# Bias rows on another DMA queue, and eight PSUM banks for the first 1024 tokens of a gated SSM + MLP kernel

## The chip, the cores and the metric

The kernel runs on one core of a Trainium2 chip. The metric is device time in microseconds (us). Every execution whose state the record gives is fast; one of 578.97 us, the first of the kernel before, is in no ratio.

In the views of the profile, PE is TensorE at its matmuls, PEld TensorE loading weights, DVE is VectorE, ACT ScalarE, POOL GpSimd and SP SyncE; a `q` behind a name is that engine's sequencer, here issuing loads. `L632` is line 632 of that run's kernel.py, and `x14` a count of instructions. A load (DMA) is issued by one of the engines and lands when its data has arrived. TensorE writes its tiles into PSUM, which the kernel uses as eight banks; to evict a tile is to copy it out of its bank, which is then free again.

## The reference

For `x` of 2048 tokens by 640 channels the kernel computes `g * a + (1 - g) * b`:

```
g = sigmoid((x * gate_w).sum(-1))
a: state space model; Lam_bar = exp(exp(log_dt) * Lam), complex, 640 states
   Bu = x @ B_bar.T ;  h_t = Lam_bar * h_{t-1} + Bu_t ;  a = 2 * Re(h @ C.T) + x * Dskip
b: MLP; gelu(x @ w1 + b1) @ w2 + b2        with w1 640 x 1728, w2 1728 x 640
```

The inputs and the output are bf16.

## The kernel before

A small list scheduler orders the instructions of each engine when the kernel is built; each operation names what it reads and writes, and waits are emitted from that. It works on 512 tokens at a time (`q` = 0 to 3). TensorE does the first layer (`m1`, lines L632 for the first seven tiles, L654 and L658 for the others), the projections to the states (`bproj`, L687), the second layer (`m2`, L762) and the output projection (`cproj`, L786). ScalarE evicts the tiles from PSUM (`ge`, L640 and L667, and `u`, L696). VectorE does the scan. The part that the change touches, with cuts marked:

```python
BK_IN = [0, 1, 2, 3]      # banks of the tiles of m1 and bproj
BK_M2 = [4, 5]
BK_C = [6, 7]
# ... cut ...
op("b1z", "pool", 0.2, (), ["b1a", ("b1b", 0), ("b1b", 1)], f_b1z, prio=-50)   # zeroes b1rows
# lre, lim, ldt (rows of the SSM's parameters) are loaded on "act"
load("b1a", "pool", "l_b1a", b1rows[0:NF - 1, :], B_b1[0:nmain]..., ["b1a"], prio=-49, dur=0.8, lat=4.0)
for h in range(2):
    load(f"b1b{h}", "pool", f"l_b1b{h}", b1rows[NF - 1:NF, ...], B_b1[nmain:F]..., [("b1b", h)], prio=-48, dur=0.8, lat=4.0)
# ... cut ...
def f_colb():             # bias rows -> columns, by a transpose on TensorE in bank 7
    return inc("pe", nc.tensor.transpose(psD[:, 0:NF], b1rows[:, :], ident[0:NF, 0:NF]))
op("colb", "pe", 0.1, ["b1a", ("b1b", 0), ("b1b", 1), "ident"], [("bank", 7)], f_colb, prio=14.5)
# ... cut: m1_first does 7 tiles of q = 0 in banks 0 to 6, 5 matmuls of 512 columns each ...
def m1(q, j0=0):
    for jf in range(j0, NF):
        bank = BK_IN[ctr["in"] % 4]
        ctr["in"] += 1
        # ... 5 matmuls into PS[bank]; then ScalarE: GELU with bias b1col -> Gl ...
def bproj(q):
    for k in range(KP):
        for ci in range(2):
            bank = BK_IN[ctr["in"] % 4]
            ctr["in"] += 1
            # ... 5 matmuls with BT into PS[bank]; then ScalarE: copy -> U ...
# ... cut ...
m1_first(); m1(0, NW); bproj(0); ssm(0); gates(0); m1(1); ssm(1); bproj(1); ...; outs(0)
```

SyncE's queue carries, in this order, two loads of `x`, five of `W1sb` (one per 128 rows, the first seven tiles' columns), ten transposing loads of `BT` (the real and the imaginary half of each of five blocks of 128 rows), then `xT`, `W2sb` and `CT`.

## Time and profile before

| | before |
|---|---|
| median of the first three runs | 218.63 us (217.95 to 578.97) |
| span of the profile | 216.5 us |
| TensorE busy, granted clock | 98%, 1.00 |
| first-layer matmuls start | 6.64 us |
| last TensorE work ends | 213.9 us |

The page of the kernel before: engines' busy time in us, then the busy share of TensorE and its granted clock in 40 slices (9 is 90% or more), then the chain that ended last, by engine.

```profile
PE 211.3 (98%) x1288; PEld 124.0 (57%) x1299; DVE 191.2 (88%) x268; ACT 100.2 (46%) x173; POOL 6.3 (3%) x17
...
PE   7899999999999999999999999999999999999995
...
PEclk9999999999999999999999999999999999999999
...
PE 95%; DMA 2%; SPq 0%; issue 0%; ACT 0%; DVE 0%
```

TensorE works without a break once it has started; only the first slice and the last are below 80%. The granted clock reads 9 in every slice and 1.00 as a mean. PE shows 1288 instructions and PEld 1299: eleven matmul records are missing from this trace.

The head of that chain, in order of time (start us, us, what):

```profile
1.77 4.74 DMA W1sb<-in_B_w_dram
...
6.64 3.18 PE ps L632 x14
```

So the first load of `W1sb`, issued at 1.77 us and landing at 6.51, releases the first layer.

The timeline of TensorE (start us, us, engine, line, operation, count, and in brackets the idle time before and what ended it):

```profile
6.64 3.18 PE L632 MATMUL ps<-xT,W1sb 128*128 128x512 bf16 x14 [0.64 <-DMA W1sb<-in_B_w_dram]
9.76 0.18 PE L450 MATMUL ps<-ident,b1rows 14*128 14x14 bf16 x1
...
14.41 6.64 PE L654 MATMUL ps<-xT,W1sb 128*128 128x512 bf16 x30
20.98 0.74 PE L658 MATMUL ps<-xT,W1sb 128*64 128x256 bf16 x10
21.88 10.74 PE L687 MATMUL ps<-xT,BT 128*128 128x512 bf16 x49 [0.16 <-ACT Gl L667]
...
58.05 2.21 PE L762 MATMUL ps<-W2sb,Gl 128*128 128x320 bf16 x15
```

The bias transpose (L450) stands at a fixed place, after 14 matmuls. The groups follow each other at the pace of their matmuls: thirty of 512 columns take 6.57 us from start to start, 219 ns each with the change to the next form. The only wait for ScalarE in this listing is the 0.16 us before the projections.

The waits (who waits for whom: us in total, times, longest):

```profile
ACT U L696 <- PE ps L687: 18.6, 40, 0.6
...
ACT Gl L667 <- PE ps L654: 16.1, 41, 0.5
...
PE ps L687 <- ACT Gl L667: 0.2, 1, 0.2
```

ScalarE waits for TensorE's tiles 81 times on the two eviction lines; TensorE waits for an eviction once.

ScalarE's timeline around its first activation and the first GELU:

```profile
2.01 1.28 ACT L460 ACT_TABLE_LOAD   x1 [2.01 <-issue]
5.37 0.21 ACT L460 ACTIVATE dtb<-lcol 128x5 bf16<-128x5 f32 x1 [2.08 <-DVE lcol L444]
...
10.23 1.28 ACT L640 ACT_TABLE_LOAD   x1 [0.76 <-DVE b1col L455]
13.32 1.27 ACT L640 ACTIVATE Gl<-ps,b1col 128x512 bf16<-128x512 f32 x2 [1.81 <-PE ps L632]
```

The GELU table is ready at 11.5 us and the first GELU waits 1.8 us more for TensorE.

### The profile page before, as it was taken

What the parts mean: (1) busy time and instruction counts of PE and PEld (TensorE: products, weight loads), DVE (VectorE), ACT (ScalarE), POOL (GpSimd) and SP (SyncE); (2) the same over time, 40 slices, a digit from 0 to 9 for tenths busy, and PEclk for the clock granted to TensorE, in tenths of its full rate; (3) what the DMA queues carried; (4) which work ended last, traced back from release to release, by engine and by line L of the source; (5) the groups of instructions that cost most, each with busy time, mean ns of one, the idle gap of its engine ahead of it and who ended that gap; (6) DMA issues with size and microseconds to landing.
All of it is one profiled execution on the core that took longest, in us unless ns stands there. A gap on an engine that the chain in (4) does not pass through costs nothing.

```text
span 216.5 us, 3305 instructions
## 1 busy us (share of the span) xinstructions
PE 211.3 (98%) x1288; PEld 124.0 (57%) x1299; DVE 191.2 (88%) x268; ACT 100.2 (46%) x173; POOL 6.3 (3%) x17
## 2 busy tenths in 40 slices
PE   7899999999999999999999999999999999999995
PEld 4344444444577776444467777444457777777773
DVE  3799999999999999999997999799999989996312
ACT  2568656675533324556643233556673233232220
POOL 4000030000000100000000010000000000000000
PEclk9999999999999999999999999999999999999999
DMA  6997599996300040000000013000000000000000
GB/s 192 275 283 125 85 304 301 178 154 131 71 3 30 30 154 0 30 0 0 3 0 11 22 46 137 30 3 0 0 3 0 30 33 0 30 30 33 30 30 30
DMA packets 28923, 15.44 MB, mean 71 GB/s; under 512 B 22126, under 2 KB 28462, under 8 KB 28910
## 3 DMA queue, kind: packets, MB, share of 16 engines
q1 hardware_dynamic: 26912, 11.88, 23.7%
q0 software_dynamic: 656, 2.30, 3.5%
q10 hardware_dynamic: 1342, 1.07, 1.7%
q8 instruction: 10, 0.16, 0.3%
q14 instruction: 3, 0.02, 0.0%
HBM read 7.38 MB, written 2.62 MB: 46 GB/s over the span
## 4 chain that ended last, share of the span: by engine, by line
PE 95%; DMA 2%; SPq 0%; issue 0%; ACT 0%; DVE 0%
PE ps L762 28%; PE ps L654 22%; PE ps L786 20%; PE ps L687 20%; PE ps L632 4%; DMA W1sb<-in_B_w_dram 2%; PE ps L658 1%; SPq L328 0%; ACT Gl L667 0%; DVE osb L819 0%; PE ps L450 0%
## 5 line engine op out<-in xcount | busy, mean ns | idle before, releaser
L762 PE MATMUL ps<-W2sb,Gl 128*128 128x320 bf16 x448 | 63.6, 299 | 0.0
L762 PEld LDWEIGHTS ps<-W2sb,Gl 128*128 128x128 bf16 x448 | 43.6, 98 | 17.5 <-issue 0.4
L654 PE MATMUL ps<-xT,W1sb 128*128 128x512 bf16 x219 | 48.4, 379 | 0.3
L786 PE MATMUL ps<-CT,H 128*128 128x320 bf16 x320 | 46.1, 299 | 0.0
L727 DVE TENSOR_TENSOR_SCAN W<-atab,V 128x1280 bf16<-128x1280 f32 x16 | 44.3, 2811 | 0.3
L687 PE MATMUL ps<-xT,BT 128*128 128x512 bf16 x196 | 43.1, 379 | 0.3 <-ACT Gl L667 0.2
L786 PEld LDWEIGHTS ps<-CT,H 128*128 128x128 bf16 x320 | 31.2, 98 | 12.3
L667 ACT ACTIVATE Gl<-ps,b1col 128x512 bf16<-128x512 f32 x45 | 30.6, 692 | 16.1 <-PE ps L654 16.1
L654 PEld LDWEIGHTS ps<-xT,W1sb 128*128 128x128 bf16 x225 | 22.0, 98 | 26.5
L687 PEld LDWEIGHTS ps<-xT,BT 128*128 128x128 bf16 x200 | 19.4, 98 | 23.2 <-issue 0.4
L696 ACT ACTIVATE U<-ps 128x512 bf16<-128x512 f32 x40 | 23.9, 597 | 18.6 <-PE ps L687 18.6
L805 DVE SCALAR_TENSOR_TENSOR xg<-xn,gcol,dsk 128x640 bf16<-128x640 bf16 x16 | 13.9, 883 | 0.4
L770 ACT ACTIVATE E_0<-ps,g1col 128x320 bf16<-128x320 f32 x12 | 6.3, 527 | 16.5 <-PE ps L762 16.5
L611 DVE SCALAR_TENSOR_TENSOR scr<-xn,gwb 128x640 bf16<-128x640 bf16 x16 | 13.2, 823 | 0.4
L506 DVE TENSOR_TENSOR H<-H,V 128x1280 bf16<-128x1280 bf16 x16 | 12.5, 821 | 0.3
L506 DVE TENSOR_TENSOR V<-V,W 128x1280 bf16<-128x1280 bf16 x16 | 12.5, 821 | 0.3
L506 DVE TENSOR_TENSOR V<-mr,U 128x2560 bf16<-128x2560 bf16 x8 | 11.9, 1489 | 0.5 <-DVE s L506 0.3
L506 DVE TENSOR_TENSOR H<-c,W 128x2560 bf16<-128x2560 bf16 x8 | 11.9, 1488 | 0.1
L506 DVE TENSOR_TENSOR V<-s,W 128x2560 bf16<-128x2560 bf16 x8 | 11.9, 1484 | 0.0
L506 DVE TENSOR_TENSOR W<-mi,U 128x2560 bf16<-128x2560 bf16 x8 | 11.9, 1484 | 0.0
L770 ACT ACTIVATE E_2<-ps,g1col 128x320 bf16<-128x320 f32 x10 | 5.3, 527 | 13.4 <-PE ps L762 13.4
L770 ACT ACTIVATE E_1<-ps,g1col 128x320 bf16<-128x320 f32 x10 | 5.3, 528 | 13.3 <-PE ps L762 13.3
(96 smaller groups left out, 114.7 us busy)
## 6 DMA issues: line engine op xcount, KB each, us to landing
out_dram<-osb SPq DMA_DIRECT2D x15, 160.0 KB, 1.8
W2sb<-in_B_w_dram SPq DMA_DIRECT2D x1, 2080.0 KB, 12.5
xn<-in_A_x_dram POOLq DMA_DIRECT2D x3, 640.0 KB, 4.7
W1sb<-in_B_w_dram SPq DMA_DIRECT2D x5, 224.0 KB, 4.9
xn<-in_A_x_dram SPq DMA_DIRECT2D x2, 320.0 KB, 3.2
W1sb<-in_B_w_dram ACTq DMA_DIRECT2D x1, 560.0 KB, 5.5
W1sb<-in_B_w_dram ACTq DMA_DIRECT2D x1, 480.0 KB, 6.5
xT<-in_A_x_dram SPq DMA_TRANSPOSE x10, 3.9
```

Of the source, the lines that this page charges most:

```text
L506: return inc("dve", nc.vector.tensor_tensor(out=o, in0=a, in1=b, op=o_))
L611: t = inc("dve", nc.vector.scalar_tensor_tensor(out=scr[:, :], in0=xn[q % 2][:, c, :], scalar=1.0, in1=gwb[:, :], op0=ALU.mult, op1=ALU.mu ...
L632: return inc("pe", nc.tensor.matmul(PS[jf][:, :], W1sb[:, k, jf * 128:(jf + 1) * 128], xT[:, k, 0:512], start=(k == 0), stop=(k == KD - 1)))
L654: t = nc.tensor.matmul(PS[bank][:, :], W1sb[:, k, jf * 128:(jf + 1) * 128], xT[:, k, q * 512:(q + 1) * 512], start=(k == 0), stop=(k == KD ...
L667: return inc("act", nc.scalar.activation(Gl[q % 2][:, jf, :], PS[bank][:, :], ACT.Gelu_apprx_tanh, bias=b1col[:, jf:jf + 1]))
L687: t = nc.tensor.matmul(PS[bank][:, :], BT[:, kd, ci, k * 128:(k + 1) * 128], xT[:, kd, q * 512:(q + 1) * 512], start=(kd == 0), stop=(kd = ...
L696: return inc("act", nc.scalar.activation(dst, src, ACT.Copy, scale=1.0 if ci == 0 else -1.0))
L727: t = inc("dve", nc.vector.tensor_tensor_scan(out=g[:, ci, :], data0=a, data1=v[:, ci, :], initial=0.0, op0=ALU.mult, op1=ALU.add))
L762: t = nc.tensor.matmul(PS[bank][:, 0:HALF], Gl[q % 2][0:n, jf, t4 * 128:(t4 + 1) * 128], W2sb[0:n, jf, cols], start=(jf == 0), stop=(jf == ...
L770: return inc("act", nc.scalar.activation(E1[c % NE][:, cols], PS[bank][:, 0:HALF], ACT.Copy, scale=g1col[:, c:c + 1]))
L786: t = nc.tensor.matmul(PS[bank][:, 0:HALF], H[b % NHB][:, ci, k, s * 128:(s + 1) * 128], CT[:, k, ci, cols], start=(i == 0), stop=(i == 2 ...
L805: return inc("dve", nc.vector.scalar_tensor_tensor(out=xg[c % 2][:, :], in0=xn[q % 2][:, c % 4, :], scalar=gcol[:, c:c + 1], in1=dsk[:, :] ...
```

## The change

The intent: bring the bias rows sooner by the quicker queue, and let TensorE run further ahead of ScalarE while the banks of the second layer are not yet in use. The whole diff:

```diff
-        load("b1a", "pool", "l_b1a", b1rows[0:NF - 1, :], ..., ["b1a"], prio=-49, dur=0.8, lat=4.0)
+        load("b1a", "act", "l_b1a", b1rows[0:NF - 1, :], ..., ["b1a"], prio=-97, dur=0.4, lat=2.5)
         for h in range(2):
-            load(f"b1b{h}", "pool", f"l_b1b{h}", ..., [("b1b", h)], prio=-48, dur=0.8, lat=4.0)
+            load(f"b1b{h}", "act", f"l_b1b{h}", ..., [("b1b", h)], prio=-96 + h, dur=0.4, lat=2.5)
 
+        def in_bank():
+            i = ctr["in"]
+            ctr["in"] += 1
+            return (7 + i) % 8 if i < 2 * (NF + 2 * KP) - NW else BK_IN[i % 4]
+
         def m1(q, j0=0):
             for jf in range(j0, NF):
-                bank = BK_IN[ctr["in"] % 4]
-                ctr["in"] += 1
+                bank = in_bank()
         # the same in bproj
```

The order of instructions on each engine, compared between the two built programs, differs in nothing but the three loads.

More of the change, by code (lines that the diff above doesn't have):

```diff
@@ L360, in bass_gated_mix__ssm_conv_s5__dense_activation_gelu__prompt_kernel @@
             load(nm, "act", "l_" + nm, rows[:, i, :], src.rearrange("(k p) -> k p", p=128), [("rows", i)], prio=-100 + i, dur=0.45)
-        load("b1a", "pool", "l_b1a", b1rows[0:NF - 1, :], B_b1[0:nmain].rearrange("(j p) -> j p", p=128), ["b1a"], prio=-49, dur=0.8, lat=4.0)
+        load("b1a", "act", "l_b1a", b1rows[0:NF - 1, :], B_b1[0:nmain].rearrange("(j p) -> j p", p=128), ["b1a"], prio=-97, dur=0.4, lat=2.5)
         for h in range(2):
-            load(f"b1b{h}", "pool", f"l_b1b{h}", b1rows[NF - 1:NF, h * 64:h * 64 + FL], B_b1[nmain:F].rearrange("(j p) -> j p", j=1), [("b1b", h)],
-                 prio=-48, dur=0.8, lat=4.0)
+            load(f"b1b{h}", "act", f"l_b1b{h}", b1rows[NF - 1:NF, h * 64:h * 64 + FL], B_b1[nmain:F].rearrange("(j p) -> j p", j=1), [("b1b", h)],
+                 prio=-96 + h, dur=0.4, lat=2.5)
         def f_iota():
@@ L680, in bproj @@
                 for ci in range(2):
-                    bank = BK_IN[ctr["in"] % 4]
-                    ctr["in"] += 1
+                    bank = in_bank()
                     def f_mm(k=k, ci=ci, bank=bank):
```

## The prediction

> **What bounds the kernel.** TensorE. The page's first part gives PE 211.3 us busy of 216.5 (98%), granted clock 1.00; VectorE 88%, ScalarE 46%. The chain that ended last is 95% PE; the W1sb load has 2.2%. The PE timeline shows work without a break from 6.64 us (first-layer matmul, released by W1sb's landing at 6.51) to 213.9 us, at full rate: 50 projection matmuls of 512 columns take 10.75 us, 215 ns each. The Trainium skill, "TensorE: Matmul & The Clock Gate", section "Wait — 56ns, not 53.3ns?", gives 215.7 ns start to start as the warm rate; this trace agrees. The matmuls sum to about 206 us (460 x 0.215, 40 x 0.067, 768 x 0.136). Head, tail and about 1 us of small breaks are the rest.
>
> **What the change does.**
> (a) Three tiny loads (3.3 KB) go from POOL to ACT. POOL loses three issues of 0.48 to 0.68 us; ACT gains three of about 0.3 us (its neighbours take 0.28 and 0.31), from 1.98 to about 2.9 us. Its first table load then ends near 4.2 us instead of 3.3; its first activation, at 5.37, waits for VectorE's lcol, so nothing moves. The bias rows land 2 us earlier, estimated; today about 7.2 (issued to 2.9, landing 4.2 later). But their transpose has a fixed place in PE's order, after 14 first-layer matmuls, at 9.76 us: they had 2 us to spare. The first GELU starts at 13.32 on PE's result, its table ready at 11.5. The skill, "DMA: Bandwidth & Descriptors", section "Issuing engines are not separate DMA queues", says that issuing from more engines saves only issue time; here that is not on the chain.
> (b) The rotation grows from four banks to eight for 41 tiles. A PE tile takes 1.08 us, its eviction 0.69 (GELU) or 0.60 us (copy): four banks already keep ahead. In the waits by engine ScalarE waits for PE (16.1 and 18.6 us on the two eviction lines), PE for ScalarE once, 0.16 us at 21.7. Even that I take for an artefact: its group has 49 of 50 records, and 50 x 0.215 from 21.65 ends at 32.4, where the next stage's first weight load (32.24) expects it. Tightest: bank 0 comes free near 18.0 us, PE wants it at 18.7.
> (c) Each engine's instruction order is the same apart from the three loads; only branches between blocks are fewer, and PE ran through those without loss.
> (d) Sharing banks 4 to 7 with second layer and output projection costs nothing: the projections use them in order, bank 4 being evicted some 2.5 us before the second layer wants it at 58 us.
>
> **Sum.** 0 to 0.3 us saved, from the doubtful break and 0.1 us around the bias transpose; W1sb's landing 0.1 to 0.2 us either way. The fast times before differ by 0.3%, more than that.
>
> Predicted: 218.3 us, 217.3 to 219.3 in 8 of 10. Faster by over 2%: 0.01; within 2%: 0.97; slower: 0.02.
>
> **What would show it.** Right: PE starts near 6.6 us; the timeline's PE groups start within 0.3 us of before throughout; PE busy near 211 us; ScalarE's waits for PE unchanged; bias rows landing near 5 us. Wrong: W1sb landing later, a PE idle entry in the 1024-token stages, or later PE groups moved by over 0.5 us.
>
> **What would make it wrong.** SP's issues slowed by ACT's, or a hidden PE stall that modelled matmul ends cover up, freed by eight banks.

## The result, and the profile after

| | before | after |
|---|---|---|
| median | 218.60 us (6 runs) | 218.24 us (217.74 to 218.75, 6 runs) |
| ratio, 95% interval | | 0.9986, 0.9964 to 1.0009 |
| span of the profile | 216.5 us | 216.6 us |
| first-layer matmuls start | 6.64 us | 6.16 us |
| projections' weights load from | 21.64 us | 21.70 us |

A ratio is the mean time of one kernel's fast runs over that of the other's of the same rounds, so it is not quite the ratio of the medians. The interval holds 1.

The page of the kernel after:

```profile
PE 212.3 (98%) x1299; PEld 124.2 (57%) x1299; DVE 191.3 (88%) x268; ACT 100.2 (46%) x173; POOL 4.8 (2%) x14
...
PE   7999999999999999999999999999999999999995
...
PE 89%; SPq 7%; DMA 2%; issue 0%; DVE 0%
```

The extra 1.0 us of PE is no extra work: the trace of after has all 1299 matmul records. POOL has lost its three issues. The chain has changed at its head, where SyncE's queue now holds 7%. In order of time its end there is:

```profile
15.42 1.28 SPq L335
...
16.75 4.91 DMA BT<-in_A_B_im_dram
```

L335 are the transposing loads of `BT`, issued one behind the other by SyncE; the last lands at 21.66 us and releases the projections. TensorE's timeline:

```profile
6.16 3.20 PE L637 MATMUL ps<-xT,W1sb 128*128 128x512 bf16 x14
9.30 0.18 PE L450 MATMUL ps<-ident,b1rows 14*128 14x14 bf16 x1
...
13.95 6.64 PE L658 MATMUL ps<-xT,W1sb 128*128 128x512 bf16 x30
20.52 0.74 PE L662 MATMUL ps<-xT,W1sb 128*64 128x256 bf16 x10
21.70 10.97 PE L690 MATMUL ps<-xT,BT 128*128 128x512 bf16 x50 [0.45 <-DMA BT<-in_A_B_im_dram]
...
58.10 2.07 PE L765 MATMUL ps<-W2sb,Gl 128*128 128x320 bf16 x14
```

This is worth reading slowly. The first layer starts 0.48 us earlier and keeps that lead to 20.52 us (20.98 before). (`W1sb` landed 0.83 us earlier, at 5.68 us, but TensorE was still at its preparation until 6.16; experiment 2 comes back to this.) Then TensorE waits 0.45 us for `BT`, and the second layer starts 0.05 us later than before. A lead was won at the head and lost 15 us later, at the next load. The question for the experiments is whether the change won that lead. The waits:

```profile
ACT U L699 <- PE ps L690: 19.1, 40, 0.7
...
ACT Gl L671 <- PE ps L658: 16.1, 41, 0.5
...
PE ps L690 <- DMA BT<-in_A_B_im_dram: 0.4, 1, 0.4
```

The GELUs wait for TensorE exactly as before (16.1 us, 41 times): the eight banks changed nothing there. The copies' 0.5 us more is the wait for `BT`, handed on. ScalarE's timeline:

```profile
2.02 0.93 ACTq L328 DMA_DIRECT2D b1rows<-in_B_b_dram  x3
2.97 1.28 ACT L460 ACT_TABLE_LOAD   x1 [2.97 <-issue]
5.48 0.21 ACT L460 ACTIVATE dtb<-lcol 128x5 bf16<-128x5 f32 x1 [1.22 <-DVE lcol L444]
...
12.86 1.27 ACT L645 ACTIVATE Gl<-ps,b1col 128x512 bf16<-128x512 f32 x2 [1.36 <-PE ps L637]
```

The three issues take 0.93 us and put the table load back by as much, into idle time. By the landing records of the two traces the last bias rows came at 6.29 us and not at 7.28; TensorE asked for them at 9.3 us and 9.8.

### The profile page after: what moved, and what is told of

Read it like the earlier page. It is cut to its first block, busy times and chain, and to the rows that moved or that the text cites. A ratio compares the mean times of both kernels' runs of the same rounds, so it can differ in the third digit from the quotient of the medians.

```text
span 216.6 us, 3320 instructions
## 1 busy us (share of the span) xinstructions
PE 212.3 (98%) x1299; PEld 124.2 (57%) x1299; DVE 191.3 (88%) x268; ACT 100.2 (46%) x173; POOL 4.8 (2%) x14
## 4 chain that ended last, share of the span: by engine, by line
PE 89%; SPq 7%; DMA 2%; issue 0%; DVE 0%
PE ps L765 28%; PE ps L789 20%; PE ps L690 20%; PE ps L658 19%; SPq L335 6%; DMA BT<-in_A_B_im_dram 2%; SPq L328 1%; PE ps L662 1%; DVE osb L822 0%
## 5 line engine op out<-in xcount | busy, mean ns | idle before, releaser
L658 PE MATMUL ps<-xT,W1sb 128*128 128x512 bf16 x225 | 49.2, 379 | 0.0
L690 PE MATMUL ps<-xT,BT 128*128 128x512 bf16 x200 | 43.8, 379 | 0.4 <-DMA BT<-in_A_B_im_dram 0.4
L671 ACT ACTIVATE Gl<-ps,b1col 128x512 bf16<-128x512 f32 x45 | 30.6, 692 | 16.1 <-PE ps L658 16.1
L506 DVE TENSOR_TENSOR V<-mr,U 128x2560 bf16<-128x2560 bf16 x8 | 11.9, 1489 | 0.5 <-DVE s L506 0.3
L506 DVE TENSOR_TENSOR H<-c,W 128x2560 bf16<-128x2560 bf16 x8 | 11.9, 1488 | 0.1
L506 DVE TENSOR_TENSOR W<-mi,U 128x2560 bf16<-128x2560 bf16 x8 | 11.9, 1485 | 0.0
L506 DVE TENSOR_TENSOR V<-s,W 128x2560 bf16<-128x2560 bf16 x8 | 11.9, 1484 | 0.0
```

The source lines that it names most:

```text
L506: return inc("dve", nc.vector.tensor_tensor(out=o, in0=a, in1=b, op=o_))
L658: t = nc.tensor.matmul(PS[bank][:, :], W1sb[:, k, jf * 128:(jf + 1) * 128], xT[:, k, q * 512:(q + 1) * 512], start=(k == 0), stop=(k == KD ...
L671: return inc("act", nc.scalar.activation(Gl[q % 2][:, jf, :], PS[bank][:, :], ACT.Gelu_apprx_tanh, bias=b1col[:, jf:jf + 1]))
L690: t = nc.tensor.matmul(PS[bank][:, :], BT[:, kd, ci, k * 128:(k + 1) * 128], xT[:, kd, q * 512:(q + 1) * 512], start=(kd == 0), stop=(kd = ...
```

## The experiments

Three theories. **Slack** (mine): TensorE's rate bounds the kernel, both parts act where there is slack, and the early start in the trace of after is scatter between executions. **Queue** (rival): POOL's loads had held `W1sb` back; the move did win 0.5 us, and the wait for `BT` hid it. **Banks** (rival): the eight banks free a stall of TensorE that the modelled matmul ends do not show. Each run was profiled, and then timed in rounds with the kernel before on the same chip (three chips in all, six executions a run, four in bias_late_a and bias_late_b). On two of the chips, those of experiments 3 to 5 and of bias_sp and bias_sp_re, the kernel before has executions near 220.5 us (220.43, 220.48, 220.55) for medians of 218.32 and 218.65; nothing here explains them, and they widen those intervals.

### 1. Each part alone: queue_only and banks_only

queue_only is the kernel before with the first hunk of the diff, banks_only with the others.

> The kernel before with the bias loads on ACT's queue and the four banks kept. Slack theory (TensorE bounds, neither part is on its chain): 218.3 us, ratio 0.997 to 1.002, W1sb's first landing anywhere from 5.6 to 6.6 us by chance. Queue theory (POOL's loads held W1sb's landing back, and the wait for BT hides the gain): W1sb lands near 5.7 us, the first-layer matmuls start near 6.15 us instead of 6.64, TensorE then waits about 0.4 us for BT near 21.3 us; the time is the same as under the slack theory. Bank theory (eight banks alone saved something): ratio 1.000, no gain here.

Measured: 217.96 us, ratio 0.9978 (0.9956 to 1.0000).

> The kernel before with the eight banks and the bias loads left on POOL's queue. Slack theory: 218.3 us, ratio 0.997 to 1.002, ScalarE's waits for TensorE unchanged (16.1 us on the GELU line). Queue theory: W1sb's first landing near 6.5 us and the first-layer start near 6.6 us, as in the trace before. Bank theory: ratio 0.9986 or lower, with TensorE groups after the 1024-token stages starting at least 0.3 us earlier relative to the first-layer start.

Measured: 218.51 us, ratio 0.9999 (0.9979 to 1.0020). TensorE's timeline of banks_only, whose bias loads are POOL's as before:

```profile
5.87 3.32 PE L637 MATMUL ps<-xT,W1sb 128*128 128x512 bf16 x14
...
21.64 10.97 PE L690 MATMUL ps<-xT,BT 128*128 128x512 bf16 x50 [0.56 <-DMA BT<-in_A_B_im_dram]
```

and of queue_only, which still has four banks:

```profile
5.73 3.20 PE L632 MATMUL ps<-xT,W1sb 128*128 128x512 bf16 x14
...
20.75 10.96 PE L687 MATMUL ps<-xT,BT 128*128 128x512 bf16 x50
```

banks_only starts early too, at 5.87 us, with the loads where they always were, and loses the lead at `BT`. So the early start does not need the queue move. queue_only got the best draw of both, `W1sb` at 5.55 us and `BT` at 19.74, and has the shortest span of all, 215.6 us. It also settles the doubtful 0.16 us before the projections: with the same four banks and all 50 records there is no such wait. In before the group had 49 records; the first one is missing, and its place looks like idle time. bias_sp below, with eight banks and again 49 records, shows the same 0.16 us.

### 2. The changed kernel again: after_again

> The changed kernel once more, for the scatter of the landings. Slack theory: W1sb's first landing and BT's last differ from the first trace (5.68 and 21.66 us) by up to 1 us, and the time is 218.3 us, ratio 0.997 to 1.001. Queue theory: W1sb lands before 6.0 us again.

Measured: 218.44 us, ratio 0.9998 (0.9979 to 1.0016). `W1sb` landed at 6.18 us and the first layer started at 6.87, the latest start of all undelayed runs, with the bias rows on ACT's queue. The queue theory had expected a landing before 6.0.

The 0.69 us between landing and start are not a wait for a load. Before the first layer TensorE does six matmuls on zeros, twenty transposes of `x` (L418) and one more matmul on zeros (L407), and in after_again these ran late. The second ten transposes and that matmul, first in after_again, then in queue_only:

```profile
5.41 1.25 PE L418 MATMUL ps<-ident,xn 128*128 128x128 bf16 x10
6.45 0.63 PE L407 MATMUL ps<-wz 128*128 128x512 bf16 x1
```

```profile
4.93 0.73 PE L418 MATMUL ps<-ident,xn 128*128 128x128 bf16 x10
5.50 0.38 PE L407 MATMUL ps<-wz 128*128 128x512 bf16 x1
```

From the first transpose to L407 a transpose takes 0.104 us in after_again (5.41 to 6.45) and 0.057 in queue_only (4.93 to 5.50). Every trace begins at the slower pace, and the moment at which it doubles, read from the matmuls' starts, differs: 4.2 to 4.8 us in four of the five traces with POOL's bias loads (bias_late_b, whose TensorE waited, is apart), 4.0 to 7.0 us in the nine others. Why is open, and single traces cannot tell chance from an effect of the change; a cost of it does not show in the times (0.9986 and 0.9998). after_again also had a late landing of the second half of `x`: 5.36 us, 4.88 in queue_only.

### 3. The suspected cost doubled: bias_twice

The kernel before with each bias load issued twice on POOL:

```diff
+ load("b1xa", "pool", ..., b1x[0:NF - 1, :], B_b1[0:nmain]..., prio=-49.9, dur=0.0, lat=0.0)   # scratch
+ for h in range(2):
+     load(f"b1xb{h}", "pool", ..., b1x[NF - 1:NF, ...], ..., prio=-49.8, dur=0.0, lat=0.0)
  load("b1a", "pool", ...)
```

> The kernel before with the three bias loads issued twice on POOL, first into a scratch tile; the real ones are issued 1.5 to 2 us later and should land near 9 us. Slack theory: TensorE asks for them 3.1 us after its start (8.9 to 10.0 us), so it waits 0 to 0.3 us at most and the time is unchanged, ratio 0.997 to 1.002, though the suspected cost is doubled. Queue theory: twice the POOL loads hold W1sb's first landing back to 7 us or later, and the first-layer start with it, ratio 1.002 to 1.005.

Measured: 218.24 us, ratio 0.9979 (0.9933 to 1.0024), so no loss. Its TensorE timeline:

```profile
5.79 3.19 PE L637 MATMUL ps<-xT,W1sb 128*128 128x512 bf16 x14
9.11 0.16 PE L455 MATMUL ps<-ident,b1rows 14*128 14x14 bf16 x1
```

With twice the loads on POOL, `W1sb` landed at 5.57 us, the second earliest of all. The queue theory had 7 us or later; it falls. The bias rows landed at 8.98 us, and their transpose came 3.32 us after the start where before has 3.12: a wait of 0.2 us, the edge of the slack.

### 4. Past the edge of the slack: bias_late_a and bias_late_b

The kernel before with one (a) or three (b) memsets of 128x2560 elements on POOL ahead of the bias rows:

```diff
+ op("dly", "pool", 0.2, (), [("H", 2), "dly"], f_dly, prio=-55)     # memset of H[2]; in b of H[0], H[1], H[2]
- op("b1z", "pool", 0.2, (), ...)
+ op("b1z", "pool", 0.2, ["dly"], ...)
```

> The kernel before, with one memset of 128x2560 elements put ahead of the bias rows on POOL, which should delay their landing (6.3 to 7.3 us in the runs so far) by 1 to 3 us. TensorE asks for them 3.1 us after its first-layer start, 8.9 to 10.0 us. Slack theory: as long as they land before about 9 us the time is unchanged, ratio 0.997 to 1.002. If the loads' landing were felt before that, the time would rise by the delay, 1 to 3 us (ratio 1.005 to 1.014).

Measured: 219.15 us, ratio 1.0036 (0.9995 to 1.0077). The memset took 2.22 us and the last rows landed at 10.75 us, so past the moment of asking, not before it as I had half expected: the rows came 3.5 us later than in before, where I had expected 1 to 3. The waits of TensorE:

```profile
PE ps L457 <- DMA b1rows<-in_B_b_dram: 1.6, 1, 1.6
```

That run started at 6.05 us, so TensorE asked at about 9.2 and waited 1.6. From there on the landing counts in full: the span of 217.7 us is 1.1 us over before's, which is the wait of 1.6 us less the 0.6 us by which this execution started earlier. The interval of the times alone does not resolve it.

> The same with three such memsets, 4 to 8 us of delay, so past the moment at which TensorE asks. Slack theory: TensorE waits before the bias transpose for landing minus 3.1 us after first-layer start, and the time rises by that wait less what BT's landing swallows (0 to 0.6 us): for a landing at 13 us about 3.5 us of wait and 3 us of time. Without a dependence at that place the time would not change.

Measured: 223.06 us, ratio 1.0217 (1.0173 to 1.0261), and a miss as an experiment: something else was delayed. VectorE's timeline:

```profile
2.36 3.33 DVE L382 CAST io_f<-io_i 128x128 f32<-128x128 int32 x1
...
5.72 2.24 DVE L385 TENSOR_SCALAR ident<-io_f 128x128 bf16<-128x128 f32 x1
```

In before these take 0.23 us each. Here they finished at 5.69 and 7.96 us, near the ends of POOL's second and third memset (2.22 us each from 1.21: 5.65 and 7.88, worked out from their total). The identity came 5.1 us late (7.96 us, 2.85 in before) and the first transpose, which needs it, 4.3 us (8.10, 3.80 in before), so the run says nothing of the bias rows. The Trainium skill, "SBUF — State Buffer", section "Who interferes with whom", says that casts and `tensor_scalar` can take ports which VectorE shares with GpSimd, and that the later of the two then fully blocks; the times here agree, and so do those of bias_late_a, where the same cast, begun at 2.36 us, ended at 3.52, just behind the one memset (1.21 to 3.43). There TensorE lost hardly anything by it: its first transpose started at 3.92 us, 3.80 in before.

### 5. Fewer banks: banks3, banks2, banks2_fixed

The changed kernel with `BK_IN[i % 3]` or `BK_IN[i % 2]` for the 41 tiles.

> The changed kernel with three banks in turn for the 41 tiles, not eight. From the trace after: the burst of seven GELUs ends 3.3 us after TensorE's first tile of the rest starts, the fourth tile needs bank 0 again 3.23 us after that start, and its GELU ends about 3.6 us after it. Slack theory: one wait of TensorE for ScalarE of 0.3 to 0.5 us there, none afterwards; the stretch from first-layer start to projections is 15.4 to 15.6 us where four and eight banks have 15.0 to 15.1 without a wait for BT; the time rises by 0 to 0.4 us, as far as BT's landing does not swallow it (ratio 0.998 to 1.003). Bank theory (bank count is always felt): a wait in most of the 41 tiles and 2 us or more in all.

Measured: 218.73 us, ratio 1.0014 (0.9980 to 1.0047). The one wait for a bank, from TensorE's timeline:

```profile
17.91 3.40 PE L658 MATMUL ps<-xT,W1sb 128*128 128x512 bf16 x15 [0.38 <-ACT Gl L671]
```

It is the fourth tile, as expected, and the stretch from first-layer start (6.36) to the projections' weights (21.90) is 15.54 us, as expected (15.0 without a wait). There is also a 0.16 us entry before its projections; that group has 49 records again.

> The changed kernel with two banks in turn for the 41 tiles. Slack theory: the third tile needs bank 0, whose second GELU can only start when the burst of seven is over; TensorE waits 1.3 to 1.7 us once; after that a tile lasts 1.08 us and its eviction 0.69 us plus about 0.2 us of signalling, so two banks keep up and no later tile waits more than 0.1 us. Stretch from first-layer start to projections 16.4 to 16.8 us, time up by 0.8 to 1.7 us (ratio 1.003 to 1.008). VectorE's gates come earlier in its order here, which should not show. Bank theory: waits in most tiles, up by 4 us or more.

Measured: 220.89 us, ratio 1.0102 (1.0063 to 1.0141), more than I had expected. TensorE's timeline has the wait after the burst, and a second one that I had not foreseen:

```profile
18.27 4.48 PE L658 MATMUL ps<-xT,W1sb 128*128 128x512 bf16 x20 [1.47 <-ACT Gl L671]
...
41.60 8.79 PE L658 MATMUL ps<-xT,W1sb 128*128 128x512 bf16 x39 [1.64 <-ACT Gl L671]
```

The scheduler, told of fewer banks, had moved VectorE's gates up, and ScalarE's tanh sat 2.15 us in front of two evictions waiting for them; the gates themselves had waited 3.15 us for the load of `gwb`. I had said that this should not show; it did. (The profiled execution was the slowest of the six, 222.35 us against 220.00 to 221.08, so the 1.64 us need not hold for the others.) banks2_fixed restores VectorE's order:

```diff
- op(f"gz{q}", "dve", ..., [("xn", q % 2, 0), ("xn", q % 2, 1), "gwb"], ...)
+ op(f"gz{q}", "dve", ..., [("xn", q % 2, 0), ("xn", q % 2, 1), "gwb"] + ([("H", 0)] if q == 0 else []), ...)
```

> Two banks again, with VectorE's first gates tied behind its first scan block, so that the order of VectorE is that of the kernel before. In the first run with two banks the order had moved the gates up, and with them ScalarE's tanh, which waited 2.15 us for VectorE and held two evictions; TensorE waited 1.64 us for that. If that is what cost the second half: the wait of 1.4 to 1.6 us after the seven-GELU burst stays (and 0.4 us at the first projections), the wait of 1.64 us near 40 us is gone, and the time is up by 1.0 to 1.9 us (ratio 1.004 to 1.009). If two banks are short in the steady state: waits stay in the second 512 tokens and the ratio stays at 1.010.

Measured: 220.23 us, ratio 1.0059 (1.0020 to 1.0098). The wait near 40 us is gone, the first one stays:

```profile
17.94 4.48 PE L658 MATMUL ps<-xT,W1sb 128*128 128x512 bf16 x20 [1.47 <-ACT Gl L671]
```

The timeline also has waits of 0.42 and 0.20 us at the two projection stages, but both groups lack records. The weight loads, whose records are complete, put the true wait at 0.24 us each: they begin 0.91 us after the first weight load of the first-layer tile before them, where four and eight banks without a wait for `BT` have 0.67. Before banks2 I had expected no later wait above 0.1 us. Apart from these, the bank count is felt where the arithmetic of tile time and eviction says, and four is enough. In before, the first GELU behind the burst of seven starts at 17.32 us and takes 0.69, so bank 0 is free again near 18.0; TensorE wants it at 18.7 with four banks, and one tile (1.08 us) earlier with three.

### 6. The next wall: re_first, bias_sp, bias_sp_re

If `BT` is what swallows an early start, the order of its halves should matter. re_first is the changed kernel with

```diff
- load_T("B", "l_B", [... for k in range(KD) for ci in range(2)], ["BT"], prio=6.8, dur=13.1)
+ for ci in range(2):
+     load_T(f"B{ci}", f"l_B{ci}", [... for k in range(KD)], [("BT", ci)], prio=6.8 + 0.01 * ci, dur=6.55)
  # bproj: the loop over ci outside, each tile waits for ("BT", ci)
```

> The changed kernel, with all real parts of BT transposed before the imaginary ones, a semaphore for each half, and the projections in that order, so that the first five projection tiles need five transposes and not ten. If the wait of 0.45 us for BT in the changed kernel's trace is what gave the early start back, that wait is gone: the projections start within 0.1 us of the end of the first layer (21.25 us after a start at 6.16, later by as much as W1sb lands later), every later TensorE group moves by 0.3 to 0.5 us and the time falls to 217.7 to 218.1 us, ratio 0.996 to 0.999. If something else bounds it later (CT, the scan), a wait appears elsewhere and the time stays at 218.3.

Measured: 218.26 us, ratio 0.9989 (0.9971 to 1.0008). No wait for `BT` appears, but this execution started at 6.59 us and its `BT` had landed whole at 21.35 us, before TensorE asked (21.59). So the profile does not test the idea, and the time, expected at 217.7 to 218.1 us, does not show a gain.

bias_sp puts the bias loads on SyncE's queue between `W1sb` and `BT` (`"sp"`, prio 6.5 to 6.7) so that `BT` should land later; bias_sp_re is the same on top of re_first.

> The changed kernel with the bias loads on SyncE's queue, between W1sb and BT. They land within the slack (7.5 to 9 us), but BT's ten transposes, issued back to back at about 1.3 us each, start about 1.3 us later. If BT's landing is the wall right behind TensorE's start: BT lands at 21.5 to 23.2 us, TensorE waits 0.5 to 1.7 us before the projections and the time rises by 0.3 to 1.3 us (ratio 1.001 to 1.006). If BT had slack as the bias rows have: no wait, ratio 0.998 to 1.001.

> The same with the real parts of BT first, as in the earlier run with that order. The first five tiles need transposes that land before 17 us; the imaginary ones are needed 5.4 us after the projections start. So the wait for BT is gone and the time is back at 218.0 to 218.4 us, ratio 0.997 to 1.001, 0.3 to 1.3 us below its sister. If the wait is not BT's last landing, both cost the same.

Measured: bias_sp 218.68 us, ratio 0.9991 (0.9947 to 1.0035), and bias_sp_re 218.65 us, ratio 0.9981 (0.9942 to 1.0021). Both expectations of a difference failed. `BT`'s first transpose was issued 1.15 us later (5.34 us, 4.19 in after), yet the last landed at 21.50 us, within the range of the other runs: the tenth was issued 11.9 us after the first, where before has 13.1 and after 12.6, so SyncE made up its delay. The bias rows themselves landed at 9.31 and 9.73 us, later than the 7.5 to 9 expected; TensorE took them at 9.88 and 9.87, so in bias_sp_re nothing was left of the slack. Both also started late (6.74 and 6.67 us), so TensorE asked at 21.7 and found `BT` there. Whether the order of the halves gains anything in an execution with an early start is left open.

### All undelayed runs side by side

Landings are from the traces' landing records; the last column is the span minus the time at which the projections' first weights load.

| run | bias queue, banks | `W1sb` first lands | first layer starts | `BT` all landed | projections' weights | span | rest |
|---|---|---|---|---|---|---|---|
| before | POOL, 4 | 6.51 | 6.64 | 20.72 | 21.64 | 216.55 | 194.9 |
| banks_only | POOL, 8 | 5.74 | 5.87 | 21.59 | 21.64 | 216.54 | 194.9 |
| bias_twice | POOL twice, 4 | 5.57 | 5.79 | 19.89 | 20.99 | 215.89 | 194.9 |
| queue_only | ACT, 4 | 5.55 | 5.73 | 19.74 | 20.75 | 215.63 | 194.9 |
| after | ACT, 8 | 5.68 | 6.16 | 21.66 | 21.70 | 216.60 | 194.9 |
| after_again | ACT, 8 | 6.18 | 6.87 | 21.75 | 21.96 | 216.86 | 194.9 |
| re_first | ACT, 8 | 6.46 | 6.59 | 21.35 | 21.59 | 216.48 | 194.9 |
| bias_sp | SyncE, 8 | 6.18 | 6.74 | 21.50 | 21.76 | 216.66 | 194.9 |
| bias_sp_re | SyncE, 8 | 6.26 | 6.67 | 21.54 | 21.74 | 216.63 | 194.9 |

Everything from the projections on takes 194.9 us, whatever the queue and with four banks or eight. What differs is the head: the projections start about 15.0 us after the first layer, or when `BT` has landed, whichever is later. The first layer starts between 5.73 and 6.87 us, and neither queue has the early starts to itself. Over all fourteen traces `W1sb` first lands at 5.57 to 6.51 us with the bias loads on POOL (five traces), at 5.55 to 6.46 on ACT (seven) and at 6.18 and 6.26 on SyncE. The start has two limits, though: it comes 0.13 us after the landing in before, banks_only and re_first, but 0.41 to 0.69 us after it in after, after_again, bias_sp and bias_sp_re, where TensorE was still at its preparation, all or part of it at half pace.

## Why the prediction was right, and where it was not

- **The time**: 218.3 us predicted, 218.24 measured; ratio 0.9986, interval 0.9964 to 1.0009. Right.
- **TensorE bounds the kernel at its full rate**: right. The rest after the projections' start is 194.9 us in all nine runs. The Trainium skill, "TensorE: Matmul & The Clock Gate", section "Wait — 56ns, not 53.3ns?", gives 215.7 ns for 512 columns; in the trace of after, which has all records, the 50 projection matmuls take 10.80 us from start to start (21.70 to 32.50), 216 ns each.
- **The bias rows had 2 us to spare**: right. Moved 1.7 us later (bias_twice, last landing 8.98 us) they cost a wait of 0.2 us in a run that started early and nothing in the time; at 10.75 us (bias_late_a) TensorE waits 1.6 us. "The bias rows land 2 us earlier" was mis-sized: it was 1.0 us (7.28 to 6.29).
- **Moving the issuer saves only issue time**, as the prediction took from the skill: right for the kernel's time, as neither engine was wanted there (POOL's issues took 0.48 to 0.68 us, ACT's 0.27 to 0.31). For the rows themselves it was not the whole: of their 1.0 us, 0.48 is issue time (the last issue ended at 2.94 us, not 3.42), and the rest is a landing 3.35 instead of 3.86 us after that.
- **Four banks keep ahead**: right, and shown by dose: in the traces three cost one wait of 0.38 us, two one of 1.47 us plus two of 0.24, eight nothing less than four (banks_only 0.9999). The 0.16 us entry is an artefact of a missing record, as argued. Sharing the second layer's banks cost nothing either: in after, the second layer shows no idle entry.
- **"W1sb's landing 0.1 to 0.2 us either way"**: the step that failed. The landing scatters by 1.0 us (5.55 to 6.51 us) between executions, and the first-layer start by 1.1 us. Nor does the landing alone set the start, as the prediction took it to: in after the start came 0.48 us behind it, when TensorE had done its preparation. So the sign that I named for being wrong, an idle entry of TensorE in the 1024-token stages, did appear, and the first-layer groups moved by 0.48 us, not within 0.3. The cause is not the change: banks_only shows both with the old queue.
- **What I had missed**: the load right behind. I gave no slack for `BT`; it was 0.9 us in before (landed 20.72, wanted 21.64) and less than nothing in after, which is why an early start there was worth nothing.

Open: why the landings scatter by 1 us, why the moment at which TensorE's pace doubles differs by 3 us and whether the change moves it, and whether the queue move alone is worth 0.1 or 0.2% (queue_only's interval ends at 1.0000; the changed kernel, with the same move, has 0.9986 and 0.9998, and bias_twice, without it, 0.9979). No version here beats both kernels beyond its interval.

## What to carry to other kernels

Where the bounding engine runs gapless at its rate, count the slack of a load or a buffer before making it faster: how long before it is wanted does it arrive, and how long before a bank is wanted is it free. A lead at the head is worth only what the next load's arrival leaves of it, so look up the next one too. And when two single traces differ at a DMA's landing, repeat the kernel before believing that the change did it: here the same program's `W1sb` landed at 5.68 and 6.18 us, and its first layer started at 6.16 and 6.87. Look as well at whether the engine that waits for the load was ready for it.

## What the Trainium skill lacked or had wrong

- "Perfetto Trace Analysis" advises to rotate groups through different PSUM banks (section "Matmuls") and to use all eight (section "Matmul Optimizations"), but gives no way to tell how many a kernel needs. Here a tile takes 1.08 us and its eviction 0.69 us: four banks are as good as eight, three wait 0.38 us once and two 1.47 us, after a burst of seven evictions, and two wait another 0.24 us at each of two projection stages.
- No page that I read speaks of the scatter of landings between executions: the same 224 KB load, issued at 1.77 us, landed anywhere from 5.55 to 6.51 us in undelayed runs.
- No page that I read warns that a missing matmul record looks like a wait: 1288 of 1299 records gave a wait of 0.16 us for ScalarE that traces with all records do not have.
- "SBUF — State Buffer", section "Who interferes with whom", says that the second engine blocks for the first one's whole instruction, and not that it can be passed over. In bias_late_a that length fits (the cast ended at 3.52 us, the memset at 3.43). In bias_late_b it was longer: a cast begun at 2.36 us, during POOL's first memset (over at about 3.43), ended at 5.69, with the second.
